# A kernel of Fourier transforms and a small network: another load order, one more condition in the plan, sums in two tasks, one root and one zero product less

## The chip, the cores and the metric

The kernel runs on 1 core of one Trainium2 chip. The metric is the device time of one execution in microseconds (us); the median of 3 runs before the change is 129.49 us (129.37 to 129.72).

A core has several engines, and each works through its own queue in order: TensorE (PE, matrix products; its weight loads are shown as PEld), VectorE (DVE), ScalarE (ACT), GpSimd (POOL) and SyncE (SP, which here issues the loads and stores). The engines wait for one another by semaphores.

## The reference

`x` is 2048 x 512 in bf16. Two functions of it are mixed row by row by a gate:

```
g = sigmoid((x * gate_w).sum(-1, keepdims=True))

# A: a filter in the frequency domain
X = rfft2(x);  X = X * (w_r + 1j * w_i);  a = irfft2(X)        # w: 2048 x 257

# B: a network over the 2048 rows, used transposed
h = layernorm(x)                    # over the 512 columns, eps 1e-5
u = gelu(h.T @ w1 + b1)             # w1: 2048 x 1792
b = (u @ w2 + b2).T                 # w2: 1792 x 2048

out = g * a + (1 - g) * b
```

## The kernel before

All of `x` is held on the chip as 16 blocks of 128 rows by 512 columns. A block is named by q and r (j = 4q + r, with q and r from 0 to 3): its partition p holds row 512q + 4p + r of `x`, so that r is the row's residue modulo 4.

**The network (B).** For each block j, the mean and variance (`bn`, L487 and L488 on DVE, for some blocks L491 and L495 on ACT), the root of the variance on ACT (`sq`, L511), its reciprocal and the normalised block `h` on DVE (`rec`, L516 to L521; for some blocks L527 on ACT). Then `m1` (L705): 14 column tiles of W1 (`ft`), each a sum over the 16 blocks j, 512 columns wide; the first seven tiles use the weights in `wa`, the others those in `wb`. ACT turns each finished sum into `gl` by gelu (L721). `m2` (L1008) is the second product, from `gl` and W2, which is loaded later into the same buffers `wa` and `wb`; ACT (`yev`, L1014) scales its sums by 1 - g, and for the last pair DVE does it (`fin`, L1021).

**The transforms (A).** These are products with tables (`ta`, `tb`, `ti`, `tg`) and short sums. For each residue r, DVE makes sums over q (`q4a` and `q4b`, L535 to L542), PE multiplies by `ta` (`fa`, L554 to L557) and ACT evicts (L560). DVE combines the residues (L571 to L604), PE multiplies by `tb` (`fb`, L653), ACT evicts (L660), and DVE sums again (L669 and on). Then the filter is applied (L781 to L841), and the way back begins: sums over four on DVE (L590, L591, L600, L601), products with `ti` on PE (`i1`, L890 to L898), which ACT evicts (L904, L906), sums on DVE (`zf`, L914 to L919; `fq`, L926 and L927), products with `tg` (`i3`, L967 to L970), which ACT evicts with the factor g (L974), and a last round of sums for each pair of blocks: `es` (L982 to L995), then the addition to the network's output (`fin2`, L1027). The `i1` products are made for each half h, residue r and table half lt; `lt` 0 uses the PSUM bank tag `fa`, `lt` 1 `fb`, each with two buffers.

**The gate.** `gw`, the row `gate_w` copied to all partitions, is multiplied into `x` on DVE (L730, four instructions), and ACT adds up each row (L735).

**The start.** While the first data is on its way, PE multiplies zeros (`warm`, L353 to L358, NWARM = 10 products). On ACT, `presq` (L360 to L362) takes the root of the constant `eps`, one element per partition, ahead of the first `sq`.

**What sets the order.** Nothing is reordered at run time. A class `Plan` takes every piece of work as a task: `add(engine, duration, function, reads, writes, prio, alloc, free, after)`. It plays the tasks through with the durations given, among ready tasks takes the one with the lowest `prio`, holds back a task whose buffer (`alloc`) is not free, and has a model of the loads' speed. The order that comes out for each engine is then written out, with semaphores for what a task reads. So a `prio`, a further entry in `reads` or another duration changes the order of a queue and nothing else.

SP issues nearly all loads, in the order of their `prio`. Behind `x` for r = 0 and 1, `wa` and `ta` for r = 0, the order before is: `wa` for r = 1, first half (448 KB), `wa` for r = 1, second half (448 KB), `ta` for r = 1 (160 KB), `x` for r = 2 (512 KB), `ta` for r = 2, `wa` for r = 2 (896 KB), `x` for r = 3, `ta` for r = 3, `wa` for r = 3, `flip`, the bias b1, `tb` (194 KB), four blocks of `wb` (512 KB each), `gw` (128 KB), `b2h` (the bias b2), and later the filter, the rest of W1, and W2. The transfers rotate over 8 lanes; a load is issued when the one eight before it has landed.

Of the kernel before, what the change touches and what calls it, by code (L numbers as in the profile page):

```python
# [16 lines left out]
P = 128  # L17
S = 2048
D = 512
# [113 lines left out]
class Plan:  # L133
# [11 lines left out]
    def add(self, eng, dur, emit, reads=(), writes=(), prio=0.0, alloc=(), free=(), nbytes=0, after=(), late=0.0):  # L145
        t = Task()
        t.late = late
        t.eng, t.dur, t.emit, t.prio = eng, dur, emit, prio
        t.alloc, t.free, t.nbytes = tuple(alloc), tuple(free), nbytes
        t.users, t.end, t.ready = [], None, 0.0  # L150
        deps = set(after)
        for k in reads:
            if k in self.last_w:
                deps.add(self.last_w[k])
            self.readers.setdefault(k, []).append(t)
        for k in writes:
            if k in self.last_w:
                deps.add(self.last_w[k])
            deps.update(self.readers.get(k, ()))
            self.last_w[k] = t  # L160
            self.readers[k] = []
        deps.discard(t)
        t.deps = deps
        self.tasks.append(t)
        return t
# [99 lines left out]
def kernel(  # L265
# [22 lines left out]

    pool = ctx.enter_context(tc.tile_pool(name="sb", bufs=1))
    psum = ctx.enter_context(tc.tile_pool(name="ps", bufs=1, space=bass.MemoryType.PSUM))  # L290
    NES = 1

    def sb(shape, dt, tag, bufs=1):
        return pool.tile(shape, dt, tag=tag, name=tag, bufs=bufs)
# [58 lines left out]
    def warm():  # L353
        pw = ps([P, D], F32, "fa", 2)
        for _ in range(NWARM):
            T.matmul(pw[:], lhsT=t["warm"][:, 0:P], rhs=t["warm"], start=True, stop=True)  # L356
    NWARM = 10
    add("PE", 0.42 * NWARM, warm, reads=["warm", "xs"], writes=["warmed"], prio=-5, alloc=["fa"], free=["fa"])  # L358

    def presq():  # L360
        A.activation(t["ombb2"][:, 0:1], t["eps"][:], ActF.Sqrt, bias=t["eps"][:, 0:1], scale=1.0)
    add("ACT", 0.05, presq, reads=["eps"], writes=["omg"], prio=-5)  # L362


    Q0 = (0, 2, 1, 3)
    for q in (0, 2):
# [5 lines left out]
    for r in range(4):  # L372
        if r == 0:
            for n, qs in enumerate(XQ):
                ld([("x", 0, q) for q in qs], lambda qs=qs: t["x"][:, qs[0]:qs[-1] + 1:2, 0, :], x4[:, qs[0]:qs[-1] + 1:2, 0, :], 131072 * len(qs), -9 + 0.1 * n)
        else:
            for qs in ((0,), (1,), (2, 3)) if r == 1 else ((0, 1, 2, 3),):
                c = slice(qs[0], qs[-1] + 1)
                ld([("x", r, q) for q in qs], lambda r=r, c=c: t["x"][:, c, r, :], x4[:, c, r, :], 131072 * len(qs), 2 * r - (3 if r == 1 else 0) + 0.01 * qs[0])
        ld([("ta", r)], lambda r=r: t["ta"][:, r, :], tabs["ta"][:, r, :], 163840, 2 * r + (0.6 if r == 1 else 0.2) if r else -0.8)  # L380

    NF = 7
    WB = (0, NF, NF + 4, NFT)
# [23 lines left out]
    def ld_bias():  # L407
        dma(t["b1b"][0:NFT], B_b1.rearrange("(t f) -> t f", f=P))
    add("SP", 0.5, ld_bias, writes=["bias"], prio=7.1, nbytes=4096, after=[a0])
    load("tb", [P, 776], BF16, tabs["tb"], 198656, prio=9)  # L410

    def ld_wb(k, q):
        def emit():
# [10 lines left out]
            add("SP", 0.5, ld_wb(k, q), writes=[("w1", k + 1, 4 * q + r) for r in range(4)], prio=10 + 12 * k + 0.1 * q,  # L424
                nbytes=131072 * (WB[k + 2] - WB[k + 1]), after=after)
    load_wb(0)
    load("gw", [P, D], BF16, gate_w[None, :].to_broadcast([P, D]), 131072, prio=14.5)

    ld(["b2h"], lambda: t["b2h"][:], B_b2.rearrange("(q p r) -> p q r", q=4, r=4), 300000, 14.6)

    wsrc = (A_w_r, A_w_i)

# [440 lines left out]
    for rs, h in ((0, 0), (0, 1), (1, 0), (1, 1)):  # L873
        for r in (rs, rs + 2):
            for lt in range(2):
                tag = ("fa", "fb")[lt]

                def i1(h=h, r=r, lt=lt, tag=tag):
                    if "zz" not in t:
                        t["zz"] = sb([P, 2, 2, 2, 2, 2, 2, P], BF16, "X")  # L880
                        t["ze"] = sb([P, 2, 2, 2, 2, L], BF16, "h")
                    p1 = t["i1", h, r, lt] = ps([P, 2, L], F32, tag, 2)
                    o, w = ti_at(r)
                    ti = t["ti"][:, o:o + w]
                    for v in range(2):
                        d = lambda c: t["B"][:, lt, r, 2 * c + v, h:L:2]
                        if r % 2:
                            for c in range(2):
                                f = (2 * c if lt == 0 else 5 - c) * P
                                T.matmul(p1[:, v], lhsT=d(c), rhs=ti[:, f:f + L], start=(c == 0), stop=(c == 1))  # L890
                        else:
                            n = 129 if r == 0 and lt == 0 else P
                            u = ti[:, 256 * lt:256 * lt + 256]
                            if n > P:
                                T.matmul(p1[:, v], lhsT=d(1), rhs=t["ti"][:, 2816:3072], start=True, stop=False)
                            else:
                                T.matmul(p1[:, v, n:], lhsT=d(1), rhs=u[:, n:], start=True, stop=True)
                            T.matmul(p1[:, v, 0:n], lhsT=d(0), rhs=u[:, 0:n], start=(n == P), stop=True)  # L898
                i1t[h, r, lt] = add("PE", mm(*([256] * 4 if r % 2 else [128] * 4)), i1, reads=[("T", lt, r % 2), "ti"], writes=[("i1", h, r, lt)], prio=3, alloc=[tag])

                def i1ev(h=h, r=r, lt=lt):
                    if r % 2:
                        o = t["zz"][:, 1, h, lt, :, :, r // 2, :]
                        A.copy(o, t["i1", h, r, lt][:].rearrange("p v (k a) -> p v k a", k=2))  # L904
                    else:
                        A.copy(t["ze"][:, h, r // 2, lt], t["i1", h, r, lt][:])  # L906
                add("ACT", act(512), i1ev, reads=[("i1", h, r, lt)] + pbk, writes=[("zz" if r % 2 else "ze", h, r, lt)], prio=1.7, free=[tag], after=[lined])

            if r % 2 == 0:
                def zf(h=h, r=r):  # L910
                    e = t["ze"][:, h, r // 2]
                    k0, k1 = (t["zz"][:, 0, h, :, :, k, r // 2, :] for k in range(2))
                    if r == 0:
                        V.tensor_copy(k0[:, :, :, 0], e[:, :, :, 0])  # L914
                        V.tensor_copy(k1[:, :, :, 0], e[:, :, :, P])
                        V.tensor_add(k0[:, :, :, 1:P], e[:, :, :, 1:P], e[:, :, :, P + 1:L])
                        V.tensor_sub(k1[:, :, :, P - 1:0:-1], e[:, :, :, 1:P], e[:, :, :, P + 1:L])
                    else:
                        V.tensor_add(k0, e[:, :, :, 0:P], e[:, :, :, P:L])  # L919
                        V.tensor_sub(k1[:, :, :, ::-1], e[:, :, :, 0:P], e[:, :, :, P:L])  # L920
                add("DVE", 2 * tt(512) + (tiny(2) if r == 0 else 0), zf, reads=[("ze", h, r, lt) for lt in range(2)], writes=[("zz", h, r, lt) for lt in range(2)], prio=3.55)

        def fq(rs=rs, h=h):
            z = xph(h)[:, 2048 * rs:2048 * rs + 2048].rearrange("p (q v n) -> p q v n", q=4, v=2)
            a, b = (t["zz"][:, rs, h, i].rearrange("p v k r a -> p k v (r a)") for i in range(2))
            V.tensor_add(z[:, 0:4:3], a, b)  # L926
            V.tensor_sub(z[:, 1:3], a[:, ::-1], b[:, ::-1])  # L927
        add("DVE", 2 * tt(1024), fq, reads=[("zz", h, r, lt) for r in (rs, rs + 2) for lt in range(2)] + [("T", 0, 0), ("T", 0, 1), ("T", 1, 0), ("T", 1, 1)],
            writes=[("z", rs, h)] + ([] if rs else ["pp" if h else "xs"]), prio=3.6)
# [27 lines left out]
    for p in range(NJ // 2):  # L957
# [22 lines left out]
            return t["tb_"][:, j0:j0 + 3:2]  # L980

        def es(p=p, j0=j0, late=late, tb2j=tb2j):  # L982
            e, s = eo_v(p), sb([P, 2, 2, 2, P], BF16, "es", NES)
            o = tb2j() if late else e
            if late:
                for i in range(2):
                    V.tensor_scalar_add(e[:, i, 0, 0:129], e[:, i, 0, 0:129], t["ombb2"][:, j0 + 2 * i:j0 + 2 * i + 1])
            o = o.rearrange("p j h (k d) -> p j (h k) d", k=2)
            V.tensor_copy(s[:, :, :, :, 0], e[:, :, :, 0:129:128].rearrange("p j h k -> p j k h"))
            V.tensor_add(s[:, :, 0, :, 1:P], e[:, :, :, 1:P], e[:, :, :, P + 1:L])  # L990
            V.tensor_sub(s[:, :, 1, :, P - 1:0:-1], e[:, :, :, 1:P], e[:, :, :, P + 1:L])
            V.tensor_add(o[:, :, 0:4:3], s[:, :, :, 0], s[:, :, :, 1])
            V.tensor_sub(o[:, :, 2:0:-1], s[:, :, :, 0], s[:, :, :, 1])
        add("DVE", tiny(1) + 4 * tt(512) + (0.3 if late else 0), es, reads=(k1 + ["omg"]) if late else [],
            writes=ko if late else k1, prio=4, alloc=["es"], free=["es"], after=gates if late else ())  # L995

        for i, j in enumerate((j0, j1)):
            n = 2 * p + i
# [77 lines left out]
```

## Time and profile before

| what | value |
|---|---|
| median of 3 runs | 129.49 us |
| the profiled execution | 129.0 us |
| its span, first to last instruction | 127.1 us |
| PE busy | 122.3 us, 756 instructions |
| DVE busy | 114.6 us, 273 instructions |
| ACT busy | 81.3 us, 165 instructions |
| POOL busy | 0.2 us, 4 instructions |
| read / written in HBM | 20.86 MB / 2.10 MB |

The profile is that of one execution, and its times count from the first instruction. The profiled execution's own time is longer than its span by what lies around the first and the last instruction. In rows of the timeline the columns are the start, the duration, the engine, the line, the operation, what is written from what, the size, how many such instructions follow one another (x), and in brackets the idle time of the engine before it, with what ended it. Products on PE overlap: each is shown with its whole way through the array, so that the distance between two starts says how long one takes, not its duration. In a table of stretches each row has the stretch, then the busy time of PE, PEld, DVE, ACT and POOL with their counts, the granted clock of PE, the share of the DMA engines, and GB/s. The chain of waits follows the work that ended last back to what released it.

### The profile page before, as it was taken

To read this page: it belongs to the slowest core of one execution; us is meant where nothing else is said; L and a number is where in the kernel's file an instruction comes from. 1 tells how busy PE (TensorE), PEld (TensorE's weight loads), DVE (VectorE), ACT (ScalarE), POOL (GpSimd) and SP (SyncE) were. 2 spreads that over 40 slices of the span, in tenths; PEclk is the share of its full clock that TensorE was granted. 3 is DMA by queue.
4 is the path that set the end of the run, shared out by engine and by line. 5 is a ranking of instruction groups with operands and counts; after the bars stand their busy time and mean duration, and the time that the engine had idled before them with its cause. 6 is when DMAs were issued, how large, how long until landed. Compare 5 with 4: busy or idle time off the path is not lost.

```text
span 127.1 us, 2153 instructions
## 1 busy us (share of the span) xinstructions
PE 122.3 (96%) x756; PEld 68.9 (54%) x756; DVE 114.6 (90%) x273; ACT 81.3 (64%) x165; POOL 0.2 (0%) x4
## 2 busy tenths in 40 slices
PE   6999999999999999999999999999989999999991
PEld 2345555555555466644445555555667767655590
DVE  2789999996999999999999999999989989999951
ACT  0973789699999999999420004722389999952200
POOL 0000000000000000000000000000000000000000
PEclk9999999999999999999999999999999999999999
DMA  2999999995548946899999900000000000006451
GB/s 69 300 355 291 382 366 368 351 325 106 122 107 256 285 96 143 200 406 415 411 409 406 398 29 0 0 5 0 3 0 0 0 5 0 0 0 248 165 211 44
DMA packets 18219, 23.12 MB, mean 182 GB/s; under 512 B 2190, under 2 KB 15904, under 8 KB 18208
## 3 DMA queue, kind: packets, MB, share of 16 engines
q1 hardware_dynamic: 17616, 22.36, 52.8%
q10 hardware_dynamic: 592, 0.62, 1.6%
q8 instruction: 6, 0.10, 0.3%
q14 instruction: 5, 0.04, 0.1%
HBM read 20.86 MB, written 2.10 MB: 181 GB/s over the span
## 4 chain that ended last, share of the span: by engine, by line
DVE 37%; PE 29%; DMA 21%; SPq 8%; issue 2%; DVEq 0%
PE acc L1008 16%; DMA wa<-in_B_w_dram 12%; SPq L306 8%; DMA gw<-in_gate_w_dram 6%; DVE x L730 4%; DVE xp L828 4%; DVE st L828 3%; DMA x<-in_A_x_dram 3%; DVE st L586 3%; PE acc L705 3%; DVE xp L833 2%; DVE xp L585 2%; DVE B L840 2%; DVE xp L834 2%; PE fb L890 1%
## 5 line engine op out<-in xcount | busy, mean ns | idle before, releaser
L705 PE MATMUL acc<-h,wb 128*128 128x512 bf16 x112 | 26.9, 379 | 0.0
L1008 PE MATMUL acc<-gl,wb 128*128 128x512 bf16 (+1 forms) x98 | 24.6, 371 | 0.0
L1008 PE MATMUL acc<-gl,wa 128*128 128x512 bf16 (+1 forms) x98 | 23.8, 371 | 0.0
L1014 ACT ACTIVATE x<-acc,ombb,omg 128x512 bf16<-128x512 f32 x12 | 9.0, 777 | 21.4 <-PE acc L1008 21.4
L1008 PEld LDWEIGHTS <-wa 128*128 128x128 bf16 x126 | 13.5, 113 | 9.9
L1008 PEld LDWEIGHTS <-wb 128*128 128x128 bf16 x126 | 13.3, 113 | 9.3
L705 PE MATMUL acc<-h,wa 128*128 128x512 bf16 x64 | 17.6, 379 | 0.0
L705 PEld LDWEIGHTS <-wb 128*128 128x128 bf16 x112 | 10.7, 98 | 10.5
L705 PEld LDWEIGHTS <-wa 128*128 128x128 bf16 x112 | 10.3, 98 | 10.4 <-issue 0.8
L487 DVE BATCH_NORM_STATS2 stats<-x 128x6 f32<-128x512 bf16 x14 | 9.5, 678 | 1.9 <-DMA x<-in_A_x_dram 1.9
L560 ACT CAST xp<-fa 128x512 bf16<-128x512 f32 x16 | 9.2, 580 | 2.0 <-PE fa L557 2.0
L735 ACT ACTIVATE x<-x 128x512 bf16<-128x512 bf16 x16 | 10.2, 692 | 0.0
L721 ACT ACTIVATE gl<-acc,b1f 128x512 bf16<-128x512 f32 x11 | 7.9, 719 | 3.5 <-PE acc L705 3.5
L705 PE MATMUL fb<-h,wa 128*128 128x512 bf16 x32 | 9.7, 379 | 0.0
L527 ACT ACTIVATE h<-x,nmr,rstd 128x512 bf16<-128x512 bf16 x11 | 8.4, 807 | 1.1 <-DVE nmr L518 1.1
L705 PE MATMUL fa<-h,wa 128*128 128x512 bf16 x16 | 5.9, 381 | 0.1
L653 PEld LDWEIGHTS <-X 128*128 128x128 bf16 x64 | 4.6, 98 | 2.5 <-DVE X L637 0.7
L974 ACT ACTIVATE B<-fa,g 128x512 bf16<-128x512 f32 x8 | 5.6, 704 | 0.2 <-PE fa L970 0.2
L730 DVE TENSOR_TENSOR x<-x,gw 128x2048 bf16<-128x2048 bf16 x4 | 4.8, 1220 | 1.1 <-DMA gw<-in_gate_w_dram 1.1
L974 ACT ACTIVATE B<-fb,g 128x512 bf16<-128x512 f32 x8 | 5.7, 712 | 0.0
L356 PE MATMUL fa<-xp 128*128 128x512 bf16 x10 | 4.4, 632 | 1.2 <-DVE xp L317 1.2
L660 ACT CAST X<-fb 128x512 bf16<-128x512 f32 x8 | 5.1, 636 | 0.0
(169 smaller groups left out, 232.8 us busy)
## 6 DMA issues: line engine op xcount, KB each, us to landing
wb<-in_B_w_dram SPq DMA_DIRECT2D x11, 512.0 KB
wa<-in_B_w_dram SPq DMA_DIRECT2D x7, 512.0 KB
wa<-in_B_w_dram SPq DMA_DIRECT2D x2, 896.0 KB
wb<-in_B_w_dram SPq DMA_DIRECT2D x4, 384.0 KB
out_dram<-x SPq DMA_DIRECT2D x3, 512.0 KB
x<-in_A_x_dram SPq DMA_DIRECT2D x2, 512.0 KB
wa<-in_B_w_dram SPq DMA_DIRECT2D x2, 448.0 KB
rot<-dft_ti SPq DMA_DIRECT2D x1, 768.0 KB
```

The lines of the kernel that those rows point to most:

```text
L306: (eng or nc.sync).dma_start(out=out_ap, in_=in_ap)
L487: V.bn_stats(out=t["stats"][:, j, :], in_=t["x"][:, j // 4, j % 4, :])
L527: add("ACT", 0.71, lambda j=j: A.activation(t["h"][:, j // 4, j % 4, :], t["x"][:, j // 4, j % 4, :], ActF.Identity, bias=t["nmr"][:, j:j ...
L560: add("ACT", act(512), lambda r=r, dq=dq: A.copy(xe(r)[:, :, :, dq, :], t["pa", r, dq][:]), reads=[("pa", r, dq)], writes=[("X", r, dq)], ...
L705: T.matmul(t["u", ft][:], lhsT=w[:, j // 4, j % 4, c * P:(c + 1) * P], rhs=t["h"][:, j // 4, j % 4, :], start=(j == jorder[0]), stop=(j == ...
L721: gelus.append(add("ACT", act(512, 1) , lambda ft=ft: A.activation(t["gl"][:, ft, :], t["u", ft][:], ActF.Gelu_apprx_tanh, bias=t["b1f"][: ...
L730: add("DVE", tt(2048), lambda r=r: V.tensor_mul(t["x"][:, :, r, :], t["x"][:, :, r, :], t["gw"][:, None, :].to_broadcast([P, 4, D])), read ...
L735: A.activation(t["x"][:, q, r, :], t["x"][:, q, r, :], ActF.Copy, accum_out=t["glog"][:, 4 * q + r:4 * q + r + 1])
L828: V.tensor_mul(o, xs, w)
L974: A.activation(eo_v(p)[:, n], t["i3", j][:], ActF.Copy, scale=t["g"][:, j:j + 1])
L1008: T.matmul(t["y", j, m][:, cs], lhsT=w[:, o, 512 * q + r:512 * q + 512:4], rhs=t["gl"][:, ft, cs], start=(ft == 0), stop=(ft == NFT - 1))
L1014: A.activation(tbuf(j).rearrange("p h d -> p (h d)"), t["y", j, 0][:], ActF.Identity, bias=t["ombb2"][:, j:j + 1], scale=t["omg"][:, j:j + 1])
```

## The change

Five edits are made together.

- **Load order.** By other priorities the SP queue after the first half of `wa` for r = 1 becomes: `x` for r = 2, `ta` for r = 1, the second half of `wa` for r = 1, `wa` for r = 2, `x` for r = 3, `ta` for r = 2, `wa` for r = 3, `flip`, the bias b1, `gw`, `ta` for r = 3, four blocks of `wb`, `tb`, `b2h`.
- **No root of a constant.** `presq` is gone. The load of ACT's table for roots stays first in ACT's queue.
- **Nine zero products** in place of ten.
- **A further condition.** In the plan the `i1` task for r = 2 also reads `("T", lt, 1)`, that is, it counts as ready only when the odd sums of the same table half are done too. In the built program PE's queue changes in one thing: the second and the third of the groups that write `fb` change places. The second is now half h = 1, r = 0, `lt` = 1, and the one for h = 0, r = 2, `lt` = 1 follows in the later place. ACT's evictions follow them. DVE makes the four `zf` sums in the order (h, r) = (0,0), (1,0), (0,2), (1,2) and then four `fq`; before, it made (0,0), (0,2), the first `fq`, (1,0), (1,2) and three `fq`.
- **Split sums.** `es` becomes two tasks, `es` (into the buffer) and `es2` (out of it), with two buffers (NES = 2). DVE's instructions are the same; from the second pair on they are ordered es, es, es2, es2, fin2, fin2 over two pairs.

```
-    NES = 1
+    NES = 2
...
-    NWARM = 10
+    NWARM = 9
     add("PE", 0.42 * NWARM, warm, reads=["warm", "xs"], writes=["warmed"], prio=-5, alloc=["fa"], free=["fa"])
-
-    def presq():
-        A.activation(t["ombb2"][:, 0:1], t["eps"][:], ActF.Sqrt, bias=t["eps"][:, 0:1], scale=1.0)
-    add("ACT", 0.05, presq, reads=["eps"], writes=["omg"], prio=-5)
...
-                ld([("x", r, q) for q in qs], ..., 131072 * len(qs), 2 * r - (3 if r == 1 else 0) + 0.01 * qs[0])
-        ld([("ta", r)], ..., 163840, 2 * r + (0.6 if r == 1 else 0.2) if r else -0.8)
+                ld([("x", r, q) for q in qs], ..., 131072 * len(qs), (0, -0.9 if len(qs) > 1 else -1 + 0.01 * qs[0], 2.503, 4.6)[r])
+        ld([("ta", r)], ..., 163840, (-0.8, 2.505, 6.3, 7.3)[r])
...
-    load("tb", [P, 776], BF16, tabs["tb"], 198656, prio=9)
+    load("tb", [P, 776], BF16, tabs["tb"], 198656, prio=14.7)
...
-    load("gw", [P, D], BF16, gate_w[None, :].to_broadcast([P, D]), 131072, prio=14.5)
+    load("gw", [P, D], BF16, gate_w[None, :].to_broadcast([P, D]), 131072, prio=7.2)
...
-    ld(["b2h"], ..., 300000, 14.6)
+    ld(["b2h"], ..., 300000, 14.9)
...
-                i1t[h, r, lt] = add("PE", ..., i1, reads=[("T", lt, r % 2), "ti"], ...)
+                i1t[h, r, lt] = add("PE", ..., i1, reads=[("T", lt, r % 2), "ti"] + ([("T", lt, 1)] if r == 2 else []), ...)
...
         def es(p=p, j0=j0, late=late, tb2j=tb2j):
-            e, s = eo_v(p), sb([P, 2, 2, 2, P], BF16, "es", NES)
-            o = tb2j() if late else e
+            e = eo_v(p)
+            s = t["es", p] = sb([P, 2, 2, 2, P], BF16, "es", NES)
             if late:
...
-            o = o.rearrange("p j h (k d) -> p j (h k) d", k=2)
             V.tensor_copy(s[:, :, :, :, 0], e[:, :, :, 0:129:128].rearrange("p j h k -> p j k h"))
             V.tensor_add(s[:, :, 0, :, 1:P], e[:, :, :, 1:P], e[:, :, :, P + 1:L])
             V.tensor_sub(s[:, :, 1, :, P - 1:0:-1], e[:, :, :, 1:P], e[:, :, :, P + 1:L])
+        add("DVE", 0.08 + 2 * tt(512) + (0.45 if late else 0), es, reads=k1 + ..., writes=[("es", p)], prio=4, alloc=["es"], ...)
+
+        def es2(p=p, late=late, tb2j=tb2j):
+            s, o = t["es", p], (tb2j() if late else eo_v(p)).rearrange("p j h (k d) -> p j (h k) d", k=2)
             V.tensor_add(o[:, :, 0:4:3], s[:, :, :, 0], s[:, :, :, 1])
             V.tensor_sub(o[:, :, 2:0:-1], s[:, :, :, 0], s[:, :, :, 1])
-        add("DVE", tiny(1) + 4 * tt(512) + (0.3 if late else 0), es, ..., writes=ko if late else k1, prio=4, alloc=["es"], free=["es"], ...)
+        add("DVE", 0.01 + 2 * tt(512), es2, reads=[("es", p)] + k1, writes=ko if late else k1, prio=4, free=["es"])
```

More of the change, by code (lines that the diff above doesn't have):

```diff
@@ L378 @@
                 c = slice(qs[0], qs[-1] + 1)
-                ld([("x", r, q) for q in qs], lambda r=r, c=c: t["x"][:, c, r, :], x4[:, c, r, :], 131072 * len(qs), 2 * r - (3 if r == 1 else 0) + 0.01 * qs[0])
-        ld([("ta", r)], lambda r=r: t["ta"][:, r, :], tabs["ta"][:, r, :], 163840, 2 * r + (0.6 if r == 1 else 0.2) if r else -0.8)
+                ld([("x", r, q) for q in qs], lambda r=r, c=c: t["x"][:, c, r, :], x4[:, c, r, :], 131072 * len(qs), (0, -0.9 if len(qs) > 1 else -1 + 0.01 * qs[0], 2.503, 4.6)[r])
+        ld([("ta", r)], lambda r=r: t["ta"][:, r, :], tabs["ta"][:, r, :], 163840, (-0.8, 2.505, 6.3, 7.3)[r])
     NF = 7
@@ L426 @@
     load_wb(0)
-    load("gw", [P, D], BF16, gate_w[None, :].to_broadcast([P, D]), 131072, prio=14.5)
-    ld(["b2h"], lambda: t["b2h"][:], B_b2.rearrange("(q p r) -> p q r", q=4, r=4), 300000, 14.6)
+    load("gw", [P, D], BF16, gate_w[None, :].to_broadcast([P, D]), 131072, prio=7.2)
+    ld(["b2h"], lambda: t["b2h"][:], B_b2.rearrange("(q p r) -> p q r", q=4, r=4), 300000, 14.9)
     wsrc = (A_w_r, A_w_i)
@@ L898, in i1 @@
                             T.matmul(p1[:, v, 0:n], lhsT=d(0), rhs=u[:, 0:n], start=(n == P), stop=True)
-                i1t[h, r, lt] = add("PE", mm(*([256] * 4 if r % 2 else [128] * 4)), i1, reads=[("T", lt, r % 2), "ti"], writes=[("i1", h, r, lt)], prio=3, alloc=[tag])
+                i1t[h, r, lt] = add("PE", mm(*([256] * 4 if r % 2 else [128] * 4)), i1, reads=[("T", lt, r % 2), "ti"] + ([("T", lt, 1)] if r == 2 else []), writes=[("i1", h, r, lt)], prio=3, alloc=[tag])
                 def i1ev(h=h, r=r, lt=lt):
@@ L991, in es @@
             V.tensor_sub(s[:, :, 1, :, P - 1:0:-1], e[:, :, :, 1:P], e[:, :, :, P + 1:L])
+        add("DVE", 0.08 + 2 * tt(512) + (0.45 if late else 0), es, reads=k1 + (["omg"] if late else []), writes=[("es", p)], prio=4, alloc=["es"],
+            after=gates if late else ())
+        def es2(p=p, late=late, tb2j=tb2j):
+            s, o = t["es", p], (tb2j() if late else eo_v(p)).rearrange("p j h (k d) -> p j (h k) d", k=2)
             V.tensor_add(o[:, :, 0:4:3], s[:, :, :, 0], s[:, :, :, 1])
             V.tensor_sub(o[:, :, 2:0:-1], s[:, :, :, 0], s[:, :, :, 1])
-        add("DVE", tiny(1) + 4 * tt(512) + (0.3 if late else 0), es, reads=(k1 + ["omg"]) if late else [],
-            writes=ko if late else k1, prio=4, alloc=["es"], free=["es"], after=gates if late else ())
+        add("DVE", 0.01 + 2 * tt(512), es2, reads=[("es", p)] + k1, writes=ko if late else k1, prio=4, free=["es"])
         for i, j in enumerate((j0, j1)):
```

## The prediction

> **What bounds the kernel now.** I read the page's head first, then the chain of waits, then a table of stretches, then the timeline of each engine around every place where TensorE (PE) stands still.
>
> ```profile
> span 127.1 us, 2153 instructions
> PE 122.3 (96%) x756; PEld 68.9 (54%) x756; DVE 114.6 (90%) x273; ACT 81.3 (64%) x165; POOL 0.2 (0%) x4
> ```
>
> PE is busy for 122.3 of 127.1 us, so the time can only fall by the moments in which PE waits, or by the ends. The chain of waits (start, duration, what) shows where the work of other engines comes late:
>
> ```profile
> 13.49 9.55 DMA wa<-in_B_w_dram
> 23.07 7.65 DMA gw<-in_gate_w_dram
> ```
>
> The last block of `wa` lands at 23.04, and `gw`, queued behind four blocks of `wb`, only at 30.72. The timeline of VectorE (DVE) and of PE say who feels it (start, duration, engine, line, operation, and in brackets the idle time before it and its releaser):
>
> ```profile
> 30.74 1.23 DVE L730 TENSOR_TENSOR x<-x,gw 128x2048 bf16<-128x2048 bf16 x1 [1.09 <-DMA gw<-in_gate_w_dram]
> ...
> 44.78 0.25 DVE L637 CAST X<-fx 128x32 bf16<-128x32 f32 x1
> ```
> ```profile
> 16.88 0.38 PE L705 MATMUL fa<-h,wa 128*128 128x512 bf16 x1
> ...
> 31.83 0.22 PE L556 MATMUL fa<-rot,gl 128*128 128x128 bf16 x1
> 31.89 0.22 PE L557 MATMUL fa<-rot,gl 128*128 128x128 bf16 x1
> ...
> 32.38 0.22 PE L556 MATMUL fa<-rot,gl 128*128 128x128 bf16 x1
> 32.69 0.23 PE L557 MATMUL fa<-rot,gl 128*128 128x128 bf16 x1
> ...
> 39.37 5.56 PE L705 MATMUL acc<-h,wb 128*128 128x512 bf16 x25
> 45.09 0.40 PE L653 MATMUL fa<-tb,X 128*128 128x128 bf16 x4 [0.16 <-DVE X L637]
> ```
>
> DVE loses 1.09 us before L730. From then on PE meets DVE's results late twice. L557 follows L556 by 0.06 in one group (31.83, 31.89) and by 0.31 in another (32.38, 32.69): a stall of 0.25 to 0.26, for the product's operand L542 of DVE. Then 25 products of L705 from 39.37, at the 0.216 us that one takes (5.56 less the last one's pipe of 0.16, over 25), leave PE free at 44.77; L653 starts at 45.09, for L637, which ends at 45.03: a stall of 0.32. A third such place is in the inverse transform:
>
> ```profile
> 93.00 0.22 PE L898 MATMUL fb<-rot,B 128*128 128x128 bf16 x1
> 93.61 0.23 PE L897 MATMUL fb<-rot,B 128*128 128x128 bf16 x1 [0.39 <-DVE B L601]
> ...
> 94.72 0.22 PE L897 MATMUL fb<-rot,B 128*128 128x128 bf16 x1
> ...
> 100.81 0.27 PE L967 MATMUL fa<-tg,xp 128*128 128x256 bf16 x1
> ```
> ```profile
> 91.06 0.69 DVE L590 TENSOR_TENSOR B<-xp 128x1024 bf16<-128x1024 bf16 x1
> ...
> 92.87 0.69 DVE L601 TENSOR_TENSOR B<-st 128x1024 bf16<-128x1024 bf16 x1
> 94.14 0.18 DVE L914 COPY X<-h 128x4 bf16<-128x4 bf16 x1 [0.59 <-ACT h L906]
> ...
> 99.17 0.68 DVE L927 TENSOR_TENSOR xp<-X 128x1024 bf16<-128x1024 bf16 x1
> ```
>
> PE's second group of `fb` starts 0.61 after L898 at 93.00, where 0.06 is usual: 0.55 lost, waiting for DVE's L601 (ends 93.56). The start of the kernel is the fourth place:
>
> ```profile
> 1.21 4.45 PE L356 MATMUL fa<-xp 128*128 128x512 bf16 x10 [1.21 <-DVE xp L317]
> 5.56 0.43 PE L705 MATMUL fa<-h,wa 128*128 128x512 bf16 x1
> ```
> ```profile
> 3.09 1.28 ACT L361 ACT_TABLE_LOAD   x1 [3.09 <-issue]
> 4.38 0.29 ACT L361 ACTIVATE ombb<-eps 128x1 f32<-128x1 f32 x1
> 4.59 0.28 ACT L511 ACTIVATE rstd<-mv,eps 128x1 f32<-128x1 f32 x1
> ```
> ```profile
> 4.12 0.18 DVE L488 BATCH_NORM_AGGREGATE mv<-stats 128x2 f32<-128x6 f32 x1
> 4.90 0.16 DVE L516 RECIPROCAL rstd<-rstd 128x1 f32<-128x1 f32 x1 [0.59 <-ACT rstd L511]
> 5.10 0.41 DVE L521 TENSOR_SCALAR h<-x,mv,rstd 128x512 bf16<-128x512 bf16 x1
> ```
>
> The first real product (5.56) follows `h` (5.10 + 0.41 = 5.51), which follows the root L511 on ScalarE (ACT), which stands behind the table load and the root of a constant, L361.
>
> **The change, part by part.**
>
> *The root of a constant.* The table load stays on ACT, first and without a wait, in the built program; only the 1-element root goes. L511 then starts at 4.38 in place of 4.59, since its statistics are there (4.12 + 0.18 = 4.30). L516, L521 and `h` follow 0.21 earlier: `h` at 5.30, PE at 5.35. Gain 0.21.
>
> *Nine zero products.* Ten run 4.45 us from 1.21, to 5.66, and the first L705 starts 0.10 before that modelled end. At 4.45/10 = 0.445 each, nine leave PE free 0.44 sooner, at about 5.12. With ten, PE would be free at 5.56 and the root's removal would gain nothing; so taking the tenth away is what lets the 0.21 through, and it has no term of its own. What it may cost is a rival below.
>
> *The load order.* SP issues almost all loads; DVE needs `gw` from 30.74 - 1.09 = 29.65, with the start's gain 29.44. The stretches (last column GB/s) give the speed of the queue:
>
> ```profile
> 10.00:20.00 10.00, 9.97 (x64) 5.55 (x63) 9.58 (x30) 7.09 (x15) 0.00 (x0) 1.00 1.03 352
> 20.00:30.00 10.00, 10.00 (x59) 5.17 (x58) 9.40 (x29) 8.62 (x15) 0.00 (x0) 1.00 1.05 317
> ```
>
> `gw` (0.13 MB) now stands right behind the last `wa`, and 0.16 MB of `ta` for r = 3, which went ahead of that `wa`, comes behind: by my estimate `gw` lands at 23.04 - 0.46 (0.16 MB at 352 GB/s) + 0.41 (0.13 MB at 317), some 23.0, far ahead of 29.44. So DVE's 1.09 goes whole, and with the 0.21 DVE is 1.30 earlier from L730 on. L542 and L637 then come 1.30 earlier at most; PE, itself earlier, waits for neither: 0.26 + 0.32, say 0.58, gained on top of 0.21, because PE's lead over the old time (0.21, 0.47, 0.79) stays below DVE's. For what is moved back: `ta` of r = 3 lands at about 23.5 and its products start near 32; `tb` lands where `gw` did, near 30.7, and L653 needs it at about 44.3; `b2h` keeps its place at the end. All nothing, the cover being 8 us and more. The half `wa` of r = 1 (second half) now stands behind `x` of r = 2 and `ta` of r = 1, 0.69 MB: 1.95 us at 352 GB/s. Between it and the last `wa` (23.04) lay 3.37 MB; at 317 and 352 GB/s that puts its landing before at 13.2 to 13.5, after at 15.1 to 15.4. PE takes it up at 16.88, after at 16.67. Nothing, with 1.3 us to spare; it is a rival.
>
> What takes some of DVE's 1.30 back is ACT, in the second transform:
>
> ```profile
> 47.17 0.62 ACT L660 CAST X<-fb 128x512 bf16<-128x512 f32 x1
> ...
> 49.03 0.69 ACT L721 ACTIVATE gl<-acc,b1f 128x512 bf16<-128x512 f32 x1 [0.27 <-PE acc L705]
> ...
> 51.98 0.65 ACT L660 CAST X<-fb 128x512 bf16<-128x512 f32 x1
> ```
> ```profile
> 48.47 0.68 DVE L669 TENSOR_TENSOR B<-X 128x1024 bf16<-128x1024 bf16 x1
> ...
> 52.66 0.69 DVE L669 TENSOR_TENSOR B<-X 128x1024 bf16<-128x1024 bf16 x1
> ```
>
> DVE's L669 reads what ACT's evictions L660 leave; the last one, 51.98 + 0.65 = 52.63, ends 0.03 before its L669 at 52.66. ACT moves only as PE feeds it: 0.47 at first, and up to 0.74 after the 0.27 before L721 at 49.03 is used up. So DVE keeps about 0.71 of its 1.30 beyond 52.66. PE keeps its 0.79, as nothing of DVE is awaited by PE up to 93.
>
> *The counted wait.* It changes only the plan: in the built program PE's second group of `fb` is now the one of the other half h, r = 0, which reads DVE's L590 (ends 91.75), and the one that needs L601 moves to the group that stood at 94.72. The 0.55 goes. The moved group would run at 94.72 - 0.79 - 0.55 = 93.38; L601 ends at 93.56 - 0.71 = 92.85. Next on ACT:
>
> ```profile
> 95.36 0.78 ACT L1014 ACTIVATE x<-acc,ombb,omg 128x512 bf16<-128x512 f32 x1 [0.24 <-PE acc L1008]
> 96.04 1.06 ACT L906 CAST h<-fb 128x512 bf16<-128x512 f32 x2
> ```
>
> The third z sum of DVE then waits for the first L906 of the pair at 96.04, behind L1014. With PE 1.34 and ACT some 1.2 earlier, that eviction ends near 95.4, DVE idles some 0.4, and the two L926/L927 that PE's L967 needs end near 99.36 (before 99.17 + 0.68 = 99.85). PE arrives at 100.81 - 1.34 = 99.47: no wait, by only 0.1. Before, there was 0.96.
>
> *The split sums.* The same five operations for each pair, now in two tasks with two buffers, alternating between pairs. No instruction more. In the last stretch
>
> ```profile
> 120.15 0.68 DVE L1027 TENSOR_TENSOR x<-x,B 128x1024 bf16<-128x1024 bf16 x1
> 121.23 0.75 DVE L1021 SCALAR_TENSOR_TENSOR x<-acc,omg,x 128x512 bf16<-128x512 f32 x1 [0.39 <-PE acc L1008]
> ```
>
> DVE waits 0.39 for PE after its last sum, so what the split gains or loses up to 0.39 is worth nothing; bounds 0 and, if the alternation delayed DVE by one whole L1027, a loss of 0.68 - 0.39 = 0.3. I take 0. The tail behind PE's last product is untouched.
>
> Sum: 0.21 + 0.58 + 0.55 = 1.34. The profiled execution took 129.0 us (span 127.1 and 1.9 around it), 0.5 below the median of the runs; 1.34 off the median 129.49 gives 128.15, rounded 128.2. The terms could reach 1.8 if the stalls of PE near 7, 12 and 17, which I left alone, shrink too.
>
> **The rivals.**
>
> *The z sums arrive late.* DVE now makes all four z sums before the first L926/L927. If they end no earlier than before, 99.85, PE's L967 starts at about 99.92 whatever PE gained, 0.89 earlier than before: 128.6. For it: the margin of 0.1. Against: DVE had 0.59 of idle time before 94.14.
>
> *The clock rises later (slower).* The zero products take 0.445 each, twice the 0.216 of later ones; the column of the granted clock says 1.00 all the same, so the row of L356 is the evidence. Full speed comes with the first real ones, 4.35 us after 1.21. With nine, PE is idle from about 5.12 to 5.35. If this gap made the chip count anew, another 4.35 us at half speed from 5.35 to 9.70 would cost 2.17; the other terms still come off (0.58 + 0.55 = 1.13), and some 0.2 of small stalls near 7 us would be covered by the slower products, so the sum is -0.21 + 2.17 - 1.13 - 0.2, a loss of 0.6: 130.1. It decides from a rise later than about 8.5. Against: 0.23 us is little beside 4.35. [...]
>
> *The half `wa` comes late.* If the exchange delays it not by 1.95 but by 4.3, PE waits 1.1 at 16.67 and the gain is gone: about 129.3. [...] Against: 1.3 us of room.
>
> *The change does nothing.* If `gw` were still late because its 128 rows, not its place, take the time, 0.58 falls away: 128.7. This joins the first rival.
>
> **How the numbers follow.** Forecast 128.2 (127.7 to 128.4): 0.60. First rival and the last, 128.6 to 128.7: 0.22. The `wa` rival, no change: 0.06. The clock, 130.1, and the split's loss with something unseen: 0.12. About 0.3% (0.39 us) is what a measurement of this kernel can tell from no change. Faster: 0.60 + 0.22 = 0.82; same 0.06; slower 0.12. The range reaches from 127.6 (all terms and some small stalls) to 129.3 (the `wa` rival), leaving out 0.12 above and a few hundredths below.
>
> **What would show it.** Right: no idle time before DVE's L730; no gap at L557 and L653; L511 right behind the table load and the first L705 near 5.35; products at 0.216 from there; no gap between the first two groups of `fb`; L967 near 99.5; span near 125.8. Wrong: PE steps of 0.43 after 5.6, idle PE near 16.7 or before L967, or an idle DVE before L669.

## The result, and the profile after

The changed kernel takes 127.77 us (median of 7 runs, 127.72 to 128.27); the kernel before took 128.93 us over the 7 runs that stand beside them (128.64 to 129.72). The ratio is 0.9903, with a 95% interval of 0.9875 to 0.9932: 1.16 us faster by the medians (0.88 to 1.61 by the interval), where 1.34 was forecast. The predicted 128.2 was reckoned from 129.49, the median of the first three runs of before alone, which lie at the upper end of the seven.

The profiled execution of the changed kernel took 128.14 us. It is one of the two longest of the seven; the other five took 127.72 to 127.82, and of those there is no trace. The head of the profile's page:

```profile
span 126.4 us, 2135 instructions
PE 121.3 (96%) x742; PEld 68.9 (55%) x755; DVE 113.9 (90%) x273; ACT 80.9 (64%) x164; POOL 0.2 (0%) x4
```

The line numbers of the changed kernel are 5 lower than those of before up to `i3` (L700 is the old L705, L725 the old L730, L516 the old L521, L962 the old L967) and 2 lower behind it. Some 13 records of products are missing from this trace, so the counts of PE are no reading.

First the table of waits of PE (engine, line, what it waited for, us in total, times, the longest). It holds nothing but the wait for the zeros at the very start; L653 and L897, which stood in it before, are gone:

```profile
engine line waited for: us in total, times, longest us
PE fa L356 <- DVE xp L317: 1.2, 1, 1.2
```

The timeline of DVE and of PE around the places that the prediction named:

```profile
29.82 1.22 DVE L725 TENSOR_TENSOR x<-x,gw 128x2048 bf16<-128x2048 bf16 x1
...
43.86 0.25 DVE L632 CAST X<-fx 128x32 bf16<-128x32 f32 x1
...
92.51 0.69 DVE L596 TENSOR_TENSOR B<-st 128x1024 bf16<-128x1024 bf16 x1
...
95.92 0.43 DVE L914 TENSOR_TENSOR X<-h 128x512 bf16<-128x512 bf16 x1 [0.41 <-ACT h L901]
...
99.07 0.68 DVE L922 TENSOR_TENSOR xp<-X 128x1024 bf16<-128x1024 bf16 x1
```
```profile
32.63 0.22 PE L551 MATMUL fa<-rot,gl 128*128 128x128 bf16 x1
32.69 0.22 PE L552 MATMUL fa<-rot,gl 128*128 128x128 bf16 x1
...
39.56 5.34 PE L700 MATMUL acc<-h,wb 128*128 128x512 bf16 x24
44.74 0.39 PE L648 MATMUL fa<-tb,X 128*128 128x128 bf16 x4
...
92.65 0.22 PE L893 MATMUL fb<-rot,B 128*128 128x128 bf16 x1
92.70 0.22 PE L892 MATMUL fb<-rot,B 128*128 128x128 bf16 x1
...
93.80 0.22 PE L892 MATMUL fb<-rot,B 128*128 128x128 bf16 x1
...
99.90 0.27 PE L962 MATMUL fa<-tg,xp 128*128 128x256 bf16 x1
...
122.81 0.55 PE L1006 MATMUL fb<-gl,wb 128*128 128x128 bf16 x7
```

DVE's product with `gw` (L725) has no idle time before it and starts at 29.82 in place of 30.74. PE's L552 follows L551 by 0.06, where 0.31 stood; L648 starts at 44.74, just when 24 products of 0.216 us from 39.56 are done (39.56 + 5.18); and the second group of `fb` follows the first by 0.05 (92.65, 92.70), where 0.61 stood. All three stalls are gone. The moved group runs at 93.80, after L596 (92.51 + 0.69 = 93.20).

The start is another matter:

```profile
4.38 0.29 ACT L506 ACTIVATE rstd<-mv,eps 128x1 f32<-128x1 f32 x1
```
```profile
4.91 0.41 DVE L516 TENSOR_SCALAR h<-x,mv,rstd 128x512 bf16<-128x512 bf16 x1
5.63 0.69 DVE L482 BATCH_NORM_STATS2 stats<-x 128x6 f32<-128x512 bf16 x1 [0.31 <-DMA x<-in_A_x_dram]
```
```profile
1.21 4.02 PE L356 MATMUL fa<-xp 128*128 128x512 bf16 x9 [1.21 <-DVE xp L317]
5.38 0.58 PE L700 MATMUL fa<-h,wa 128*128 128x512 bf16 x1
5.75 1.58 PE L700 MATMUL acc<-h,wa 128*128 128x512 bf16 x4
7.17 0.59 PE L700 MATMUL fb<-h,wa 128*128 128x512 bf16 x2
7.60 0.38 PE L700 MATMUL fa<-h,wa 128*128 128x512 bf16 x1
```

And the same rows of PE in the kernel before:

```profile
5.83 1.03 PE L705 MATMUL acc<-h,wa 128*128 128x512 bf16 x4
6.69 0.59 PE L705 MATMUL fb<-h,wa 128*128 128x512 bf16 x2
7.35 0.38 PE L705 MATMUL fa<-h,wa 128*128 128x512 bf16 x1
...
123.72 0.55 PE L1008 MATMUL fb<-gl,wb 128*128 128x128 bf16 x7
```

The root on ACT, `h` and the first real product come just as forecast (4.38, 4.91, 5.38). But the next four products take 1.42 us (5.75 to 7.17) where they took 0.86 (5.83 to 6.69): most of them ran at the half speed of the zero products (0.427 us from start to start, where 0.216 is full speed). The change from the one distance to the other is what I call the rise of the clock. That it is the clock is my reading and not shown: the column of the granted clock stands at 1.00 from 0.00 to 5.50, from 5.50 to 10.00 and in every later stretch. I call the seven products that use the first block `h` the first row, and the product that opens the next block the second row. The second row starts at 7.60, not before 7.35 as hoped but 0.25 after it.

From there to PE's last group, the kernel before takes 123.72 - 7.35 = 116.37 us and the changed one 122.81 - 7.60 = 115.21: 1.16 less, against the three stalls' 0.26 + 0.32 + 0.55 = 1.13. So in the two profiled executions the change gained 1.16 and lost 0.25 at the start. The times alone can't show that loss: their interval holds 1.34 as well as 1.13.

### The profile page after: what moved, and what is told of

It is laid out like the page before. It is cut to its first block, busy times and chain, and to the rows that moved or that the text cites. A ratio compares the mean times of both kernels' runs of the same rounds, so it can differ in the third digit from the quotient of the medians.

```text
span 126.4 us, 2135 instructions
## 1 busy us (share of the span) xinstructions
PE 121.3 (96%) x742; PEld 68.9 (55%) x755; DVE 113.9 (90%) x273; ACT 80.9 (64%) x164; POOL 0.2 (0%) x4
## 4 chain that ended last, share of the span: by engine, by line
PE 72%; DMA 16%; SPq 8%; issue 1%; DVE 0%
PE acc L1006 32%; PE acc L700 20%; DMA wa<-in_B_w_dram 12%; SPq L306 8%; PE fb L1006 5%; DMA wt<-in_A_w_r_dram 5%; PE fb L648 2%; PE fa L648 2%; PE fa L885 2%; PE fb L885 1%; PE fb L700 1%; PE fb L962 1%; PE fa L962 1%; PE fa L1006 1%; PE fa L549 0%
## 5 line engine op out<-in xcount | busy, mean ns | idle before, releaser
L700 PE MATMUL acc<-h,wb 128*128 128x512 bf16 x108 | 25.9, 379 | 0.1
L1006 PE MATMUL acc<-gl,wb 128*128 128x512 bf16 (+1 forms) x94 | 23.9, 371 | 0.2
L700 PE MATMUL acc<-h,wa 128*128 128x512 bf16 x62 | 17.7, 389 | 0.1
L700 PEld LDWEIGHTS <-wb 128*128 128x128 bf16 x112 | 10.7, 98 | 10.5
L700 PEld LDWEIGHTS <-wa 128*128 128x128 bf16 x112 | 10.4, 99 | 11.0 <-issue 1.0
L730 ACT ACTIVATE x<-x 128x512 bf16<-128x512 bf16 x16 | 10.2, 691 | 0.0
L700 PE MATMUL fb<-h,wa 128*128 128x512 bf16 x31 | 9.5, 379 | 0.1
L700 PE MATMUL fa<-h,wa 128*128 128x512 bf16 x16 | 6.1, 392 | 0.2
L648 PEld LDWEIGHTS <-X 128*128 128x128 bf16 x64 | 4.7, 98 | 2.1
L506 ACT ACTIVATE rstd<-mv,eps 128x1 f32<-128x1 f32 (+1 forms) x11 | 3.2, 295 | 2.7 <-DVE mv L483 2.5
```

The lines of the kernel that those rows point to most:

```text
L648: T.matmul(pb[:, k % 2, k // 2], lhsT=t["X"][:, lt, EX[e], c, k, :], rhs=tbl(k, c), start=True, stop=True)
L700: T.matmul(t["u", ft][:], lhsT=w[:, j // 4, j % 4, c * P:(c + 1) * P], rhs=t["h"][:, j // 4, j % 4, :], start=(j == jorder[0]), stop=(j == ...
L730: A.activation(t["x"][:, q, r, :], t["x"][:, q, r, :], ActF.Copy, accum_out=t["glog"][:, 4 * q + r:4 * q + r + 1])
L1006: T.matmul(t["y", j, m][:, cs], lhsT=w[:, o, 512 * q + r:512 * q + 512:4], rhs=t["gl"][:, ft, cs], start=(ft == 0), stop=(ft == NFT - 1))
```

## The experiments

The parts were first tried alone on the kernel before, all on one chip; the kernel before took 129.29 us (median) beside them.

### The load order alone

The edit is the five priorities of loads:

```
x    2 * r - (3 if r == 1 else 0) + ...          ->  (0, -0.9 or -1 + ..., 2.503, 4.6)[r]
ta   2 * r + (0.6 if r == 1 else 0.2) or -0.8    ->  (-0.8, 2.505, 6.3, 7.3)[r]
tb   9 -> 14.7        gw   14.5 -> 7.2        b2h   14.6 -> 14.9
```

> The kernel before with the new load order alone. Theory (own stalls): gw lands near 23, DVE has no idle time before L730 and comes 1.1 us earlier, the stalls of PE at L557 (0.26) and L653 (0.32) go, and the time falls by 0.58 us (0.45%). Rival (the gain needs the other parts): L601 and the z sums hold PE at 93 and 100 wherever it comes from, so that the stall at 93 grows from 0.55 to 0.8 or more and the time falls by under 0.3 us.

Measured: 128.35 us, ratio 0.9933 (0.9910 to 0.9956). PE in the profile:

```profile
5.77 0.39 PE L705 MATMUL fa<-h,wa 128*128 128x512 bf16 x1 [0.74 <-DMA wa<-in_B_w_dram]
...
8.26 0.38 PE L705 MATMUL fa<-h,wa 128*128 128x512 bf16 x1 [0.81 <-DVE h L521]
...
93.91 0.23 PE L897 MATMUL fb<-rot,B 128*128 128x128 bf16 x1 [0.39 <-DVE B L601]
```

The stalls at L557 and L653 are gone (L556 starts at 33.29 and L557 at 33.34, and L653 has no idle time before it at 45.40), and the one at 93 is as long as before, so the gain does not need the other parts. It is worth 0.67% or some 0.87 us (0.57 to 1.16). This execution also shows an unlucky start: the first weights and a block of `x` landed late, and the second row began at 8.26.

### gw alone

```
tb   9 -> 14.7        gw   14.5 -> 7.2        b2h   14.6 -> 14.9
```

This and the next three ran later, beside a kernel before of 129.57 us.

> The kernel before with gw ahead of wb and tb behind it, all other loads in the old order. Theory (gw is what DVE waits for): as good as the whole load order, 0.6 to 0.9 us faster than the kernel before (ratio 0.993 to 0.995), with no idle time of DVE before L730. Rival (the earlier x and ta count too): at most half of that.

Measured: 128.62 us, ratio 0.9933 (0.9908 to 0.9959), the same as with all loads in the new order. DVE's L730 has no idle time before it:

```profile
30.00 1.22 DVE L730 TENSOR_TENSOR x<-x,gw 128x2048 bf16<-128x2048 bf16 x1
```

(In its profile PE meets two other short waits, 0.25 near 13 us for the statistics of a block and 0.39 at 67 us for a block of W2, which no other profile shows.) So it is the place of `gw`, with `tb` behind the four blocks of `wb`, that counts; the earlier `x` and `ta` bring nothing that can be measured.

### The counted wait alone

```
-  reads=[("T", lt, r % 2), "ti"]
+  reads=[("T", lt, r % 2), "ti"] + ([("T", lt, 1)] if r == 2 else [])
```

> The kernel before with the counted wait alone. Theory (own stalls): the gap of 0.55 us between the first two groups of fb goes, PE's L967 comes 0.55 us earlier and the time falls by 0.55 us (0.43%). Rival (late sums): DVE is not earlier, the z sums now stand ahead of the first L926/L927, and PE waits before L967 for 0.3 to 0.5 us: the time falls by 0.2 us or less.

Measured: 128.67 us, ratio 0.9952 (0.9921 to 0.9984), 0.62 us (0.21 to 1.02) at 129.29. The gap between the first two groups of `fb` is gone:

```profile
93.30 0.22 PE L898 MATMUL fb<-rot,B 128*128 128x128 bf16 x1
93.35 0.22 PE L897 MATMUL fb<-rot,B 128*128 128x128 bf16 x1
```

PE does not wait before L967 either: the second L926/L927 pair of DVE ends at 100.40 and L967 starts at 100.54. The rival of late sums falls. DVE's wait for `gw` was only 0.62 in this execution, and PE, late from the start, met neither of the stalls that follow from it; the table under "What all profiles say together" comes back to that.

### The start alone

```
-    NWARM = 10
+    NWARM = 9
...
-    add("ACT", 0.05, presq, reads=["eps"], writes=["omg"], prio=-5)
```

> The kernel before without the root of a constant and with nine zero products. Theory (the gw load holds DVE): whatever PE gains at the start (0.2 us) or loses by a later rise of the clock (0.25 us), it meets again at L557, where DVE waits for gw until 30.7: the time moves by less than 0.1 us either way. Rival (the start counts in full): 0.2 us faster, or, with products at 0.43 us until 6.9, 0.25 us slower.

Measured: 129.66 us, ratio 1.0013 (0.9981 to 1.0045): no change. As expected, DVE still waits for `gw`:

```profile
31.23 1.23 DVE L725 TENSOR_TENSOR x<-x,gw 128x2048 bf16<-128x2048 bf16 x1 [1.02 <-DMA gw<-in_gate_w_dram]
```

This run cannot say whether the start is worth anything once `gw` is early; a later one was made for that.

### The split sums alone

```
-    NES = 1
+    NES = 2
...
-  one task es: copy, add, sub, add, sub
+  two tasks: es (copy, add, sub) and es2 (add, sub)
```

> The kernel before with the split sums and two buffers alone. Theory: DVE still waits for PE before its last L1021, so the time does not move (within 0.1 us). Rival (the alternation of pairs delays the sums): the idle time before L1021 goes, and the time grows by up to 0.3 us.

Measured: 129.31 us, ratio 1.0006 (0.9971 to 1.0041): no change. DVE's last wait shows why (for before it is the row with 0.39 in the prediction):

```profile
121.68 0.75 DVE L1024 SCALAR_TENSOR_TENSOR x<-acc,omg,x 128x512 bf16<-128x512 f32 x1 [1.52 <-PE acc L1011]
```

DVE's last addition to the output starts at 119.47 in place of 120.15, 0.68 earlier, and PE comes 0.46 later (its last group starts at 124.18 in place of 123.72), as `gw` landed later in this execution. The two together are the 1.1 us that DVE waits longer. What DVE gains by the split can be read from its queue: before, the first sum out of the buffer (L992) starts 0.53 after the last one into it (111.78, 112.31), and with the sums of another pair between them each instruction follows the last by 0.33 or 0.34 (L990 at 114.62, L996 at 114.96).

The four ratios together, 0.67% + 0.48% - 0.13% - 0.06%, make 0.96% faster; the whole change made 0.97%. So close a match is luck, since each part is known to 0.2 to 0.35% only. It shows no part that needs or hinders another, and could not show one worth a few tenths of a microsecond.

### The number of zero products

Four kernels on one chip, beside a kernel before of 129.15 us: the changed kernel once more, and the same with ten, twelve and seven zero products (`NWARM = 9` to 10, 12, 7).

> The changed kernel itself, for comparison with the three that follow on the same chip. Expected 1.0 to 1.3 us faster than the kernel before. [...]

> The changed kernel with ten zero products. Theory gap (PE must be kept busy up to its first real product, or the clock rises later): full speed by 5.7, the first row of products ends 0.4 us sooner, and the time is 0.2 to 0.45 us below that of the changed kernel. [...]

> The changed kernel with twelve zero products. Theory gap: the rise comes near 5.7, inside the zero products; the first real product starts near 6.0, and the second row of products (which waits for h near 7.15) starts near 7.5, so that the time is between that with nine and that with ten. Rival: 0.3 to 0.6 us slower than with nine, since the first real product starts that much later and the clock is no better.

> The changed kernel with seven zero products: PE idles from 4.2 to 5.4. Theory gap: the rise comes later than with nine, beyond 7, and the time is 0.3 to 1.0 us above that with nine. [...]

| zero products | median us | ratio to before | interval |
|---|---|---|---|
| 9 | 128.14 | 0.9902 | 0.9863 to 0.9941 |
| 10 | 128.31 | 0.9914 | 0.9883 to 0.9945 |
| 12 | 128.42 | 0.9928 | 0.9895 to 0.9961 |
| 7 | 128.70 | 0.9952 | 0.9916 to 0.9988 |

Ten came out 0.17 us slower than nine by the medians, where my theory that nine let the clock rise late has them 0.2 to 0.45 faster; the intervals overlap, so the times alone do not refute it. The profiles speak against it. The first rows of the profile with nine, this time, and of that with ten:

```profile
5.40 0.44 PE L700 MATMUL fa<-h,wa 128*128 128x512 bf16 x1 [0.17 <-DVE h L516]
5.68 1.03 PE L700 MATMUL acc<-h,wa 128*128 128x512 bf16 x4
...
7.59 0.38 PE L700 MATMUL fa<-h,wa 128*128 128x512 bf16 x1 [0.46 <-DVE h L516]
```
```profile
5.46 0.63 PE L700 MATMUL fa<-h,wa 128*128 128x512 bf16 x1
5.88 1.29 PE L700 MATMUL acc<-h,wa 128*128 128x512 bf16 x4
...
7.43 0.38 PE L700 MATMUL fa<-h,wa 128*128 128x512 bf16 x1
```

With nine the four products after the first took 0.86 us, full speed; with ten 1.12 (5.88 to 7.00), though PE had no idle time before them: full speed came at about 6.4, where the theory has it by 5.7. So nine products can have full speed early and ten can have it late, and the theory falls. With twelve it came at about 6.7, where 5.7 was expected, and the second row started at 8.02 in place of 7.5. The kernel with nine is late for another reason here: PE waits 0.46 for `h`, because a block of `x` landed late. In this execution DVE stood 0.79 us before its second statistics:

```profile
6.14 0.69 DVE L482 BATCH_NORM_STATS2 stats<-x 128x6 f32<-128x512 bf16 x1 [0.79 <-DMA x<-in_A_x_dram]
```

Seven come out 0.56 us above nine by the medians, but the intervals overlap, and in the profile with seven the products run at full speed from the first real one at 5.59. That seven are too few is likely by the times and not shown by the trace.

### The old start put back, and one wait more taken away

Three kernels beside `gw` alone: the changed kernel a third time; the changed kernel with the root of the constant and ten zero products (`presq` back, `NWARM = 10`); and the changed kernel with one line of the plan changed:

```
-  add("ACT", act(512), lambda r=r, dq=dq: A.copy(xe(r)[...], t["pa", r, dq][:]), ...)
+  add("ACT", act(512) + (0.15 if r < 2 else 0), lambda r=r, dq=dq: A.copy(xe(r)[...], t["pa", r, dq][:]), ...)
```

> The changed kernel again, as the measure for the two that follow: 0.990 of the kernel before.

> The changed kernel with the root of the constant and ten zero products put back. Theory (now that nothing of DVE masks it, the start counts): 0.1 to 0.2 us slower than the changed kernel. Rival (the landing of the first blocks of x and wa sets the start): the same within 0.1 us.

> The changed kernel with 0.15 us more in the plan for ACT's first two sets of evictions L555, which puts one more product of L700 between the transform products near 12 us, where PE waits 0.19 us for the bank that ACT frees. Theory (every wait of PE counts now): the stall of 0.19 goes and the time falls by 0.1 to 0.3 us against the changed kernel. Rival (the wait moves): the stall turns up at the next place where PE waits for ACT or DVE, and the time is the same within 0.1 us.

The changed kernel took 128.15 us (ratio 0.9898, 0.9866 to 0.9931), the one with the old start 127.74 (0.9876, 0.9850 to 0.9902), the one with the later evictions 127.86 (0.9888, 0.9855 to 0.9920). The intervals overlap, so none is shown to be faster than the changed kernel. That the new start is worth 0.1 to 0.2 us is not borne out, and whether it costs something (0.41 by these medians) stays open. In the profile of the kernel with the later evictions everything falls into place at the start:

```profile
1.21 3.65 PE L356 MATMUL fa<-xp 128*128 128x512 bf16 x9 [1.21 <-DVE xp L317]
5.40 0.39 PE L700 MATMUL fa<-h,wa 128*128 128x512 bf16 x1 [0.54 <-DMA wa<-in_B_w_dram]
...
7.16 0.38 PE L700 MATMUL fa<-h,wa 128*128 128x512 bf16 x1
...
122.36 0.55 PE L1006 MATMUL fb<-gl,wb 128*128 128x128 bf16 x7
```

Its nine zero products end at 4.86 and not at 5.23, so the last of them already ran at full speed, and PE's rest of more than half a microsecond behind them (0.54, from 4.86 to 5.40) did not bring the half speed back: the next product starts 0.22 after it, at 5.62. The second row starts at 7.16, which is 0.19 before the 7.35 of the old start: here, and in no other of these profiles, the gain of the root is seen. But from the second row to the last group it needs 115.20 us, exactly what the changed kernel needs (115.21). The stall that the edit was to take away is 0.19 in the changed kernel (PE free at 12.46, the transform products start at 12.65), and nothing of it arrives at the end: as far as the time goes, the rival holds. Where PE loses it again is not shown.

### What all profiles say together

For every profile of the changed kernel and its variants, the start of the second row and of PE's last group, from the timeline:

| kernel | second row | last group | between |
|---|---|---|---|
| changed | 7.60 | 122.81 | 115.21 |
| changed, again | 7.59 | 122.80 | 115.21 |
| changed, third | 7.63 | 122.84 | 115.21 |
| ten zero products | 7.43 | 122.64 | 115.21 |
| twelve | 8.02 | 123.22 | 115.20 |
| seven | 7.56 | 122.77 | 115.21 |
| old start | 7.35 | 122.55 | 115.20 |
| later evictions | 7.16 | 122.36 | 115.20 |

Behind the second row the changed kernel is a clockwork. What differs from one profiled execution to the next lies in its first 8 us, apart from some 0.2 us in the last stores (span less the start of the last group: 3.3 to 3.6).

The four profiles in which `gw` is late keep another time. In them the last group follows the first product with `gw` (L730, or L725 with the start alone), which DVE starts when `gw` lands:

| kernel | second row | first product with `gw` | last group | between the last two |
|---|---|---|---|---|
| before | 7.35 | 30.74 | 123.72 | 92.98 |
| split sums alone | 7.35 | 31.22 | 124.18 | 92.96 |
| start alone | 7.93 | 31.23 | 124.21 | 92.98 |
| counted wait alone | 8.13 | 31.04 | 123.45 | 92.41 |

The second row varies by 0.78 us here, and the end does not follow it; it follows `gw` to 0.02 us, less the 0.55 that the counted wait takes away. So with `gw` late the start is hidden, as the expectation for the start alone has it, and only with `gw` early does each tenth at the start count in full. It also says what the late `gw` costs PE: from the second row to the last group, beyond the 115.21 of the changed kernel and, except with the counted wait, the 0.55 at 93 us, it is 0.61, 1.07, 0.52 and 0.11 us in the order of the table. The later PE comes from the start, the less of it is left.

## Why the prediction was right, and where not

**The load order** was right in mechanism: no idle time before DVE's L730, both stalls of PE gone, and between the profiled executions close to the 0.58 us forecast (0.61 from the second row to the last group: 116.37 before, 115.76 with the load order alone). As a median it was worth 0.87 us (0.57 to 1.16), more, though the interval just holds 0.58. The term was taken from one execution in which `gw` held DVE for 1.09 us; that wait was 0.62 with the counted wait alone, 1.02 with the start alone and 1.58 with the split sums alone, where `gw` was as late as before. A wait for a load has a spread, and one profile shows one draw of it; what it costs PE ran from 0.11 to 1.07 us in these four executions, so that 0.58 was met by some luck. The half `wa` that went behind `x` did not hold PE in any profile of the changed kernel.

**DVE's reserve.** I had DVE keep 0.71 us beyond 52.66, so that L601 ends at 92.85, and the sums that L967 needs at 99.36 with PE arriving at 99.47. As PE was late by the start, ACT and DVE were too: 93.20, 99.75 and 99.90. The idle time before the third z sum is 0.41, where 0.4 was worked out, and the margin before L967 is 0.15, where 0.1 was. The rival of the late z sums did not come true.

**The counted wait** was right in place and size: 0.55 in the profile, 0.62 (0.21 to 1.02) alone.

**The split sums** were rightly put at nothing; DVE came out 1.1 us ahead there, which I had not worked out, and waited.

**The root and the zero products** are the step that failed: 0.21 was to reach PE's first product and all that follows. In the profiled execution it did reach the first product (5.38), and was lost before the second row, which came 0.25 later than before (7.60 for 7.35). Over all profiles of kernels with nine products and without the root, only the one with the later evictions kept it (7.16). The working followed one chain, root to `h` to first product, and took for granted that the next six products run at full speed and the next `h` is there. Two more things had to come right, and each did in some executions only. One is the rise of the clock, by 6.9 us in the changed kernel's profile, which makes 0.25 later than before out of 0.21 earlier. The other is the landing of the first blocks of `x`, on which DVE's second statistics wait. Why the clock and the landing differ from one execution to the next stays open. One smaller reading was off too: the working has ten zero products hold PE until 5.56. At 0.427 us from start to start they hold it until 5.48, and with ten and without the root the first product started at 5.46. So the tenth stood in the way of some 0.1 us, not of 0.2.

**The rival of the clock** had the right place, the wrong size and a cause that the profiles do not bear out. Half speed from 5.38 to 6.9 is not a count begun anew, which would have lasted to 9.70, and nine products in place of ten do not bring it on by themselves, as the executions with nine show that were at full speed by 4.9 and by 5.6, and the one with ten that was not until 6.4. Whether nine make a late rise more frequent, single profiles cannot say. The moment of the rise varies: in the changed kernel alone it lies at 5.5 and twice at 6.9 us, over all its relatives between 4.3 and 6.9. Why it varies, no run here shows.

## What to carry to other kernels

A small load that an engine needs is worth putting ahead of the large ones in its queue, and what it costs is to be looked for on another engine too: `gw`, 0.13 MB behind 2 MB, cost PE two stalls by way of DVE (0.26 and 0.32 us), 2 and 14 us after it landed. While `gw` set the time here, what came ahead of it could not be seen: the second row varied by 0.78 us, and the end followed `gw` to 0.02, less the 0.55 of the counted wait. When a plan sets the order, a stall can be removed by letting the plan see what the hardware waits for anyway, so that another group takes the place (0.55 us here). A gain at the start is only a gain if every chain that the first microseconds hang on moves with it: here 0.21 earlier at the first product was 0.25 later at the second row. Take several executions before believing 0.2 us there.

## What had not been expected of the hardware

The moment at which the distance between the starts of two products falls from 0.427 to 0.216 us, the rise of the clock as I read it, varied by 2.6 us between executions of these kernels. It came at about 4.3 (load order alone, ten products), 4.4 (later evictions, nine), 5.5 (changed, again, nine), 5.7 (before and split sums, ten), 6.4 (ten), 6.5 (start alone, nine), 6.7 (twelve) and 6.9 (changed, twice, nine). The table of stretches of the changed kernel gives a granted clock of 1.00 for the first 5.5 us all the same:

```profile
0.00:5.50 5.50, 4.15 (x10) 1.35 (x11) 2.13 (x8) 2.37 (x5) 0.20 (x4) 1.00 0.53 149
```

The landing of the first blocks varied too: DVE's second statistics, which read a block of `x` of 0.13 MB, started between 5.63 (changed) and 6.80 (load order alone) where DVE waited for that block, and at 5.47 with the old start put back, where it did not have to wait. Why is not shown; the same loads are issued in the same order up to there in all these kernels.
